# Routed experts on one core: where expert 0's ids are stored, where expert 1's rows are transposed, the order of the output rows, and how two items of the dense layer share TensorE

## The chip, the cores and the metric

The program runs on one core of a Trainium2 chip. The metric is the device time of one execution in microseconds; the kernel before was timed three times, and the median is used. One further execution was recorded by the hardware profiler, and everything read from a trace comes from that one.

## The reference

The reference has three stages, and only the last one is returned.

1. Attention over 4 batches, 8 heads, 576 positions and 64 values per head, with a causal window of 64 positions.
2. A mixture of 8 experts over the 2304 tokens of 512 values. Each token goes to exactly one expert and each expert takes exactly 288 tokens: the pairs of token and expert are walked in order of falling gate logit, and a pair is taken if the token is free and the expert is not full. Expert e computes `max(x @ w1[e], 0) @ w2[e]`, with 1024 hidden values.
3. A dense layer over all tokens: `h = x @ w_in` with 2048 hidden values, `g = max(0.01 * h, h)` (a leaky ReLU), and `g @ w_out`.

## The kernel before

**Stages.** Attention writes its rows to a scratch tensor in DRAM (`xd`). Then a router works in eight phases: phase ph finds the next expert to be filled and the ids of its 288 tokens (`r_ids`, three columns of 96). A phase is a long chain of small VectorE operations and small matmuls (tile `rp`): six rounds of a search for a threshold, and then the ids. "Expert 0" below is the one that phase 0 finds, and so on.

**Items.** Everything after the attention is one list of items, `seq`: expert 0 and expert 1 (8 items each, one per 128 hidden values), block m0 of the dense layer (16 items, one per 128 hidden values, over 512 slots), experts 2 and 3, m1, experts 4 and 5, m2, experts 6 and 7, m3, and m4 with the last 256 slots. A slot is a place in the order expert by expert: expert n fills slots 288n to 288n+287. So m2 (slots 1024 to 1535) needs only the first 96 slots of expert 5, and m3 (1536 to 2047) only the first 32 of expert 7. Expert outputs are kept transposed in `Y`, a ring of 1024 slots in two halves of 512, each with four tiles of 128 features. Where an expert's slots cross from one half into the other, `parts` (line 533) cuts them in two.

**Precision.** Each float is held as two parts, high and low, and a product is made of three matmuls: high by high, low by high, high by low. ScalarE writes the high part (a cast) and VectorE the low part (a subtraction). So for an item of the dense layer `hprod` issues 12 matmuls (4 feature tiles by 3), of which 4 read the low part of `Y`; `hstep` issues what is left of the 12 and then the activation; `ystep` issues the item's second product. Expert 0 alone works on whole floats, in 4 matmuls per step.

**Order.** The loop in `run` (line 877) writes every engine's instructions in program order: at item i the first product of item i+1 (`hstep(i + 1)`), then the second product of item i (`ystep(i)`). Weights come by `load_raw` (SyncE's queue; five buffers `raw`) and `split` (high and low part, two items ahead). A model of the engines' clocks (`Clocks`, line 973) decides, at each `tick` between matmuls, which pieces of the router's phase and of the conversion of the dense layer's weights (`Convert`, line 546) are written next. Engines run their own queues in order.

**From expert 0 to expert 1.** `gather_x(1)` issues three indirect loads of 96 rows each on GpSimd (tiles `xg`), and `xtrans(1, a)` transposes one of them on TensorE into `xtp`, from which ScalarE writes the high part and VectorE the low part of `xT`. The tile that `a = 0` and `a = 2` use is the same buffer. In this kernel all of that is written after expert 0's last second product (`ystep(7)`): in the branch `elif i + 1 == first[1]` of `run` come `R.finish(1)`, the gather, three loads on GpSimd's queue, three splits, the three transposes and `lows()` (the low parts of expert 0's output). The earlier branch, with the transposes two items ahead, is taken only if the ids are there by item 5.

**Ids for the output.** `put_ids(n)` (line 705) stores expert n's 288 ids, 4 bytes each, to the DRAM tensor `idl` by SyncE's queue, at item 4 of the expert (lines 910 and 911). Each block of the dense layer loads 512 of them at its ninth item, for the scatter of its output rows.

**End of an expert.** In `ystep`, `rows(0)` writes the high parts of the expert's output to `Y`, part by part and feature tile by feature tile, and `rows(1)` the low parts. The parts are sorted by falling length (line 828).

**Start of a block.** After an expert, `run` writes 8 products of the block's first item (none of them reads a low part of `Y`), then `PAIR` = 6 products of the second item, then the last 4 of the first item with its activation, then the other 6 of the second item, and then the first item's second product (`oa`), which reads the activation's result.

Of the kernel before, what the change touches and what calls it, by code (L numbers as in the profile page):

```python
# [623 lines left out]

FORCE, LEAD = 4, 10
XM = 4, 3, 2
PAIR = 6
ELOW, MLOW = 1, 1
WARM, CVG = 11, 2
XW = 5200  # L630
class Moe:
# [163 lines left out]
    def ystep(self, i):  # L795
        nc = self.nc
        kind, n, p, f = self.seq[i]
        self.route.flush(i)
        if kind == "m" and i == len(self.seq) - 2:
            return  # L800
        w, hh = self.w[i, 1], self.h[i]
        last = 7 if kind == "e" else 15
        st, sp = p == 0, p == last
        if kind == "e":
            if st:
                self.acc = [self.pp.tile([128, 288], F32, tag="acc", name=f"ya{n}_{d}", bufs=4) for d in range(4)]
            def prods(low):
                if n == 0:
                    for d in range(4):
                        nc.tensor.matmul(self.acc[d], w[:, 128 * d:128 * d + 128], hh[:, 0, :288].bitcast(F32), start=st, stop=sp)  # L810
                        self.route.tick()
                    return
                whi, wlo = w[:, 0], w[:, 1]
                for d in range(4):
                    a, b = whi[:, 128 * d:128 * d + 128], wlo[:, 128 * d:128 * d + 128]
                    for x, r in ((a, 0), (b, 0), (a, 1)):
                        if low is None or low == r:
                            nc.tensor.matmul(self.acc[d], x, hh[:, r, :288], start=st and x is a and r == 0, stop=sp and r == 1)
                    self.route.tick()
            if ELOW and not sp and n:  # L820
                prods(0)
                prods(1)
            else:
                prods(None)
            if sp:

                cut = [(s - 288 * n, pos, c) for s, pos, c in parts(288 * n, 288)]
                cut.sort(key=lambda x: -x[2])
                def rows(low, acc=self.acc):
                    for s, pos, c in cut:  # L830
                        for d in range(4):
                            hi, lo = (y[d][pos // 512][:, pos % 512:pos % 512 + c] for y in self.Y)
                            src = acc[d][:, s:s + c]
                            if low:
                                nc.vector.tensor_tensor(out=lo, in0=src, in1=hi.bitcast(F32), op=ALU.subtract)
                            else:
                                nc.scalar.copy(hi, src)
                rows(0)
                if n:
                    rows(1)  # L840
                else:

                    self.lows = lambda: rows(1)
        else:
            s0, N = self.mslots(n)
            nt = N // 128
            if st:
                self.acc = [self.pp.tile([128, 512], F32, tag="acc", name=f"oa{n}_{t}", bufs=4) for t in range(nt)]
            if p == 8:
                idx = self.wk.tile([128, 4], I32, tag="sidx", name=f"sidx{n}")  # L850
                nc.sync.dma_start(idx[:, :nt], self.idl[s0:s0 + N, :].rearrange("(t p) o -> p (t o)", p=128))
                self.sidx = idx
            if MLOW and not sp:
                for low in range(2):
                    for t in range(nt):
                        self.oprod(i, t, low)
                        if t % 2 or low == 0:
                            self.route.tick()
                return
            for t in range(nt):  # L860
                if i == len(self.seq) - 1:
                    self.oprod(i - 1, t)
                self.oprod(i, t)
                self.route.tick()
                if sp:
                    o = self.conv.pool.tile([128, 2, 512], F32, tag="cv_in", name=f"ot{n}_{t}", bufs=4)[:, 0, :]
                    if t % 2 == 0:
                        nc.vector.tensor_copy(o, self.acc[t])
                    else:
                        nc.scalar.copy(o, self.acc[t])  # L870
                    nc.gpsimd.memset(self.spacer, 0.0)
                    sc = nc.gpsimd.indirect_dma_start(out=self.out, out_offset=bass.IndirectOffsetOnAxis(ap=self.sidx[:, t:t + 1], axis=0), in_=o, in_offset=None)
                    for q in self.scats:
                        self.tc.declare_no_dep(sc.ins, q.ins, reason="rows of other tokens")
                    self.scats.append(sc)

    def run(self):
# [3 lines left out]
        def known():  # L881
            self.conv.hold = True
            for i in range(2):
                self.load_raw(i)
        R.finish(0, known)
        self.gather_x(0)
        for i in range(2, 5):
# [16 lines left out]
        for i in range(n):  # L904

            R.goal = 2 * (i - 16 + LEAD)
            nxt = seq[i + 1] if i + 1 < n else None
            yfirst = nxt is not None and nxt[2] == 0 and seq[i][0] == "e"
            R.goal = min(R.goal, 32)
            if seq[i][0] == "e" and seq[i][2] == 4:  # L910
                self.put_ids(seq[i][1])
            for m in range(1, 8):
                if m == 1 and not (self.ng == 2 and self.soon or 'ids' in R.out.get(1, ()) and i <= first[1] - 3):
                    continue
                self.soon |= m == 1
                if i == first[m] - FORCE and m > 1:
                    R.finish(m)
                if m == self.ng and 'ids' in R.out.get(m, ()) and i >= first[m - 1]:
                    self.gather_x(m)
                    self.ng += 1  # L920
                for a in range(3):
                    if i == first[m] - XM[a] and seq[i][0] == "m":
                        self.xtrans(m, a)
                if i == first[m] - 1 and seq[i][0] == "e":
                    self.xtrans(m, 2)
            if i == 2:

                self.conv.hold = False
                while len(self.conv.st) < 3:
                    self.conv.load()  # L930

            for j in range(i + 1, i + 6 if self.ng > 1 else min(i + 6, first[1] + 2)):
                self.load_raw(j)
            if yfirst:
                self.ystep(i)
                if i + 1 == first[1] and self.soon:
                    self.lows()
                elif i + 1 == first[1]:

                    R.finish(1, lambda: [self.load_raw(j) for j in range(i + 1, i + 3)])  # L940
                    self.gather_x(1)
                    self.ng = 2
                    for j in range(i + 3, i + 6):
                        self.load_raw(j, nc.gpsimd)
                    for j in range(i + 1, i + 3):
                        self.split(j, 0)
                    self.split(i + 1, 1)
                    for a in range(3):
                        self.xtrans(1, a)
                    self.lows()  # L950
                self.split(i + 3, 0)
                self.split(i + 2, 1)
                if PAIR and nxt[0] == "m":

                    self.hprod(i + 1, 8)
                    self.hprod(i + 2, PAIR)
                self.hstep(i + 1)
            else:
                self.split(i + 3, 0)
                self.split(i + 2, 1)  # L960
                if i + 1 not in self.h:
                    self.hstep(i + 1)
                if i == n - 3:
                    self.hstep(i + 2)
                x = [m for m in first if m > 1 - self.soon and first[m] == i + 2]
                if x and seq[i][0] == "e":
                    self.xtrans(x[0], 0)
                    self.xtrans(x[0], 1)
                self.ystep(i)
# [75 lines left out]
class RouteDriver:  # L1045
# [4 lines left out]
    EARLY, SPARE = 150, 700  # L1050
    def __init__(self, nc, router, conv):
        self.nc, self.r, self.conv, self.out, self.ph, self.g = nc, router, conv, {}, 0, None
        self.ready, self.mode, self.nfill, self.jobs, self.goal = 0, 'd', 0, [], 0
    def lighter(self):

        nc = self.nc
# [1 line left out]
    def piece(self):  # L1058
# [5 lines left out]
        try:  # L1064
            self.mode, self.nfill = next(self.g)
            self.ready = self.nc.last + self.FWD
        except StopIteration:
            self.g = None
            self.ph += 1
# [127 lines left out]
```

## Time and profile before

| what | value |
|---|---|
| times of three runs | 853.68, 855.95, 858.48 us; median 855.95 us |
| profiled execution | 850.8 us; its span from first to last instruction is 849.1 us |
| VectorE busy | 487.2 us (57%) |
| ScalarE busy | 316.2 us (37%) |
| GpSimd busy | 127.4 us (15%) |
| mean granted TensorE clock | 0.974 |

The span starts with the first instruction. The attention ends about 120 us into it, expert 0 runs from about 155 us, expert 1 from about 202 us, m0 from about 235 us, m1 from 397 us, m2 from 564 us, m3 from 708 us. Times of rows are us from the start of the span. A row of the timeline shows a run of like instructions: its start, how long it took, engine, operation, output and inputs, and in brackets the idle time before it and what ended that. Ends of matmuls are modelled, so that the next matmul may start before the end shown.

### The profile page before, as it was taken

The numbers are of one execution on the slowest core, as the hardware profiler recorded it, in microseconds if no ns is written. First come the engines' busy times: TensorE is split into PE (matmuls) and PEld (weight loads), VectorE is DVE, ScalarE is ACT, GpSimd is POOL, SyncE is SP. The second block draws the span as 40 slices with busy tenths as digits, with TensorE's granted clock in tenths as the row PEclk, the third lists the DMA queues.
The fourth block names the chain that finished last, engine by engine and source line by source line (L and its number), as shares of the span: only waits on it lengthen the run. The fifth ranks groups of instructions, "written<-read, shape, count | busy, mean of one in ns | idle before, by whom it ended". The sixth has DMA issues, their size and how long they took to land.

```text
span 849.1 us, 15411 instructions
## 1 busy us (share of the span) xinstructions
PE 795.3 (94%) x5877; PEld 654.7 (77%) x5877; DVE 487.2 (57%) x1381; ACT 316.2 (37%) x707; POOL 127.4 (15%) x147
## 2 busy tenths in 40 slices
PE   6998873998999999999999999999999999999996
PEld 4766652577977778888777778988888998888895
DVE  3799888577776877878665685322223322222332
ACT  3677742125225754342211134531124452212222
POOL 2111110210010001100000008620003770000100
PEclk9999985898999999999999999999999999999999
DMA  9999822478014985936314327581343935323662
GB/s 289 315 315 262 281 76 76 127 167 273 12 29 150 343 306 176 161 109 208 94 50 149 102 98 151 179 223 52 124 159 114 230 79 216 99 100 107 241 199 99
DMA packets 47417, 138.78 MB, mean 163 GB/s; under 512 B 10096, under 2 KB 10736, under 8 KB 47344
## 3 DMA queue, kind: packets, MB, share of 16 engines
q1 hardware_dynamic: 43072, 124.79, 47.9%
q0 software_dynamic: 3840, 12.59, 4.6%
q8 instruction: 46, 0.75, 0.5%
q10 hardware_dynamic: 432, 0.43, 0.1%
q14 instruction: 27, 0.22, 0.1%
HBM read 117.85 MB, written 19.93 MB: 162 GB/s over the span
## 4 chain that ended last, share of the span: by engine, by line
PE 51%; issue 5%; DMA 5%; DVE 5%; ACT 2%; POOL 0%; POOLq 0%; SPq 0%; DVEq 0%; ACTq 0%
PE h L1042 24%; PE oa L1042 17%; PE ya L1042 7%; PE rp L1042 2%; DMA xg<-xd,r_ids 1%; DMA idl<-r_ids 1%; DVE w L1042 1%; DMA out_dram<-ot,sidx 1%; PE xtp L1042 1%; DVE h L1042 1%; DVE hh L1042 1%; DMA sidx<-idl 1%; DMA w<-wsp 0%; DMA raw<-in_w_dram 0%; DVE r_ob L1042 0%
## 5 line engine op out<-in xcount | busy, mean ns | idle before, releaser
L1042 PE MATMUL h<-Y,w 128*128 128x512 f32 (+1 forms) x600 | 138.6, 376 | 0.0
L1042 PE MATMUL oa<-w,hh 128*128 128x512 f32 x540 | 135.0, 394 | 0.0
L1042 DVE SCALAR_TENSOR_TENSOR h<-h,tg 128x512 f32<-128x512 f32 (+1 forms) x80 | 51.5, 644 | 138.8 <-ACT tg L1042 138.4
L1042 ACT COPY tg<-h 128x512 f32<-128x512 f32 (+1 forms) x80 | 43.5, 544 | 218.0 <-PE h L1042 218.0
L1042 PEld LDWEIGHTS h<-Y,w 128*128 128x128 f32 x600 | 104.0, 188 | 20.6
L1042 PEld LDWEIGHTS oa<-w,hh 128*128 128x128 f32 x540 | 99.5, 188 | 20.8
L1042 PE MATMUL h<-xT,w 128*128 128x288 f32 x672 | 103.5, 302 | 0.6 <-ACT xT L1042 0.6
L1042 PE MATMUL ya<-hh,w 128*128 128x288 f32 x672 | 100.1, 297 | 0.5 <-DVE hh L1042 0.5
L1042 PEld LDWEIGHTS h<-xT,w 128*128 128x128 f32 x672 | 94.6, 192 | 2.7 <-issue 0.9
L1042 PEld LDWEIGHTS ya<-hh,w 128*128 128x128 f32 x672 | 91.7, 188 | 0.9 <-DVE hh L1042 0.7
L1042 PE MATMUL h<-Y,res 128*128 128x512 f32 (+1 forms) x360 | 83.6, 376 | 1.1 <-ACT Y L1042 1.1
L1042 PE MATMUL oa<-res,hh 128*128 128x512 f32 x324 | 82.1, 397 | 2.1 <-ACT hh L1042 2.1
L1042 ACT ACTIVATE hh<-h 128x288 fp32r<-128x288 f32 (+1 forms) x64 | 26.3, 411 | 132.9 <-PE h L1042 129.3
L1042 PEld LDWEIGHTS h<-Y,res 128*128 128x128 f32 x360 | 62.4, 188 | 14.0 <-ACT Y L1042 1.6
L1042 POOL TENSOR_TENSOR w<-raw,w 128x512 fp32r<-128x512 f32 x45 | 56.8, 1288 | 107.9 <-ACT w L1042 107.9
L1042 DVE TENSOR_TENSOR hh<-h,hh 128x512 fp32r<-128x512 f32 (+1 forms) x80 | 50.9, 637 | 37.6 <-ACT hh L1042 37.6
L1042 PEld LDWEIGHTS oa<-res,hh 128*128 128x128 f32 x324 | 59.3, 188 | 16.0 <-ACT hh L1042 3.8
L1042 POOL DMA_INDIRECT out_dram<-ot,sidx x18 | 18.4, 1022 | 333.1 <-DVE ot L1042 126.4
L1042 ACT CAST hh<-h 128x512 fp32r<-128x512 f32 (+1 forms) x80 | 43.5, 544 | 64.3 <-DVE h L1042 64.3
L1042 ACT CAST w<-raw 128x512 fp32r<-128x512 f32 x112 | 63.9, 619 | 2.0 <-DMA raw<-in_w_dram 2.0
L1042 DVE SCALAR_TENSOR_TENSOR hh<-h,hh 128x288 fp32r<-128x288 f32 x56 | 25.3, 454 | 53.4 <-ACT hh L1042 53.2
L1042 POOL DMA_INDIRECT xg<-xd,r_ids x24 | 26.7, 1113 | 146.5 <-DVE r_ac L1042 136.3
(150 smaller groups left out, 965.7 us busy)
## 6 DMA issues: line engine op xcount, KB each, us to landing
w<-wsp SPq DMA_DIRECT2D x80, 512.0 KB, 4.4
raw<-in_w_dram SPq DMA_DIRECT2D x58, 512.0 KB, 5.0
cv_in<-in_wio_dram SPq DMA_DIRECT2D x32, 512.0 KB, 6.3
wsp<-w SPq DMA_DIRECT2D x20, 512.0 KB, 3.8
aq<-in_q_dram SPq DMA_DIRECT2D x12, 384.0 KB, 6.2
avt<-in_vt_dram SPq DMA_DIRECT2D x12, 384.0 KB, 6.8
xd<-ax SPq DMA_DIRECT2D x18, 256.0 KB, 3.9
ak<-in_k_dram SPq DMA_DIRECT2D x8, 512.0 KB, 5.8
```

The lines of the kernel that those rows point to most:

```text
L1042: return f(*a, **kw)
```

## The change

- Expert 0's ids are stored at item 4 of expert 1, and expert 1's own at its item 6; the other experts' stay at their item 4.
- As soon as phase 1 has its ids, a hook in `RouteDriver.piece` writes the gather of expert 1's rows. If that has happened by item 6, three splits of expert 1's weights follow the first product of item 7, two transposes are written ahead of `ystep(6)`, the third ahead of `ystep(7)`, and `lows()` right after `ystep(7)`. Items 10 to 12 are then loaded by SyncE's queue and not by GpSimd's.
- The parts of an expert's output are written in the order of the slots and not by length.
- `PAIR` is 2 and not 6: 8 products of the first item, 2 of the second, 4 of the first, 10 of the second.

```diff
-PAIR = 6
+PAIR = 2
@@ in ystep
-                cut.sort(key=lambda x: -x[2])
+                cut.sort()
@@ in run
+        def rows():
+            self.gather_x(1)
+            self.ng = 2
+        R.hook = rows
         R.finish(0, known)
@@
-            if seq[i][0] == "e" and seq[i][2] == 4:
-                self.put_ids(seq[i][1])
+            if seq[i][0] == "e" and seq[i][1] and seq[i][2] in (4, 6):
+
+                if seq[i][2] == 4 or seq[i][1] == 1:
+                    self.put_ids(0 if seq[i][1] == 1 and seq[i][2] == 4 else seq[i][1])
             for m in range(1, 8):
-                if m == 1 and not (self.ng == 2 and self.soon or 'ids' in R.out.get(1, ()) and i <= first[1] - 3):
+                if m == 1 and not self.soon:
                     continue
-                self.soon |= m == 1
@@
+            if i == first[1] - 2:
+
+                self.hstep(i + 1)
+                self.soon = self.ng == 2
+                self.split(i + 2, 0)
+                self.split(i + 2, 1)
+                self.split(i + 3, 0)
             if yfirst:
@@ in the branch for ids that are not there
                     R.finish(1, lambda: [self.load_raw(j) for j in range(i + 1, i + 3)])
-                    self.gather_x(1)
-                    self.ng = 2
@@
-                if i + 1 not in self.h:
+                if i + 1 not in self.h and i != first[1] - 2:
                     self.hstep(i + 1)
@@ in RouteDriver.piece
             self.ready = self.nc.last + self.FWD
+            if self.hook and self.ph == 1 and 'ids' in self.out.get(1, ()):
+                self.hook()
+                self.hook = None
```

## Rows read from the trace of the kernel before

**Rows 1.** The profile's page, busy time of the engines (share of the span, instructions).
```profile
PE 795.3 (94%) x5877; PEld 654.7 (77%) x5877; DVE 487.2 (57%) x1381; ACT 316.2 (37%) x707; POOL 127.4 (15%) x147
```
**Rows 2.** Waits of TensorE, whole span: us in total, times, longest.
```profile
PE oa L1042 <- ACT hh L1042: 2.1, 4, 0.6
...
PE xtp L1042 <- DMA xg<-xd,r_ids: 1.6, 2, 1.0
...
PE h L1042 <- ACT Y L1042: 1.1, 2, 0.6
```
**Rows 3.** Timeline of TensorE from expert 0's last items to expert 1's first.
```profile
193.25 0.65 PE L1042 MATMUL ya<-hh,raw 128*128 128x288 f32 x2
...
193.94 3.66 PE L1042 MATMUL ya<-hh,raw 128*128 128x288 f32 x14
197.53 0.75 PE L1042 MATMUL rp<-r_oh,r_ge 128*63 128x8 bf16 x18
198.21 0.88 PE L1042 MATMUL xtp<-cft,xg 96*128 96x96 f32 x8
201.00 0.90 PE L1042 MATMUL xtp<-cft,xg 96*128 96x96 f32 x4 [1.91 <-DVE xT L1042]
202.47 5.57 PE L1042 MATMUL h<-xT,w 128*128 128x288 f32 x24 [0.57 <-ACT xT L1042]
207.88 1.35 PE L1042 MATMUL ya<-hh,w 128*128 128x288 f32 x9
```
**Rows 4.** Timeline of TensorE from expert 5's last item into m2.
```profile
560.51 3.32 PE L1042 MATMUL ya<-hh,w 128*128 128x288 f32 x24
564.38 2.13 PE L1042 MATMUL h<-Y,res 128*128 128x512 f32 x8 [0.55 <-ACT Y L1042]
...
568.68 1.56 PE L1042 MATMUL h<-Y,w 128*128 128x512 f32 x6
570.87 3.03 PE L1042 MATMUL oa<-res,hh 128*128 128x512 f32 x12 [0.63 <-ACT hh L1042]
```
**Rows 5.** Two stretches: busy time of each engine, then TensorE's granted clock (PEclk), DMA share, GB/s.
```profile
204.00:205.00 1.00, 1.00 (x6) 1.00 (x5) 1.00 (x4) 0.00 (x0) 0.00 (x0) 0.50 0.06 25
360.00:362.00 2.00, 0.98 (x7) 0.56 (x6) 1.83 (x7) 0.89 (x2) 0.00 (x0) 1.00 1.00 307
```
**Rows 6.** Timeline of ScalarE and of VectorE between the two experts.
```profile
197.93 1.66 ACT L1042 CAST w<-raw 128x512 fp32r<-128x512 f32 x3
199.50 0.86 ACT L1042 CAST xT<-xtp 128x384 fp32r<-128x384 f32 x2
...
198.59 1.89 DVE L1042 TENSOR_TENSOR w<-raw,w 128x512 fp32r<-128x512 f32 x3 [1.40 <-ACT w L1042]
200.40 1.01 DVE L1042 TENSOR_TENSOR xT<-xtp,xT 128x384 fp32r<-128x384 f32 x2
```
**Rows 7.** Timeline of GpSimd, the first gather of expert 1's rows.
```profile
186.99 0.98 POOL L1042 DMA_INDIRECT xg<-xd,r_ids  x1 [33.05 <-DVE r_ac L1042]
```
**Rows 8.** DMA issues in windows at 177, 182, 187 and 151 us: KB, us to landing.
```profile
idl<-r_ids SPq DMA_DIRECT2D x1, 1.1 KB, 10.5
...
raw<-in_w_dram SPq DMA_DIRECT2D x1, 512.0 KB, 9.3
...
xg<-xd,r_ids POOLq DMA_INDIRECT x1, 9.0
...
xg<-xd,r_ids POOLq DMA_INDIRECT x1, 3.2
```
**Rows 9.** Timeline of ScalarE and VectorE at the same crossing: the parts of expert 5's output.
```profile
562.68 2.07 ACT L1042 CAST Y<-ya 128x192 fp32r<-128x192 f32 x8 [1.57 <-PE ya L1042]
...
564.36 1.81 DVE L1042 TENSOR_TENSOR Y<-ya,Y 128x192 fp32r<-128x192 f32 x8 [2.75 <-ACT Y L1042]
```
**Rows 10.** Timeline of TensorE late in m0: two rounds of the router's phase 3.
```profile
316.91 0.61 PE L1042 MATMUL rp<-r_oh,r_ge 128*31 128x8 bf16 x18
...
322.96 0.61 PE L1042 MATMUL rp<-r_oh,r_ge 128*31 128x8 bf16 x18
```

More of the change, by code (lines that the diff above doesn't have):

```diff
@@ L1052, in __init__ @@
         self.nc, self.r, self.conv, self.out, self.ph, self.g = nc, router, conv, {}, 0, None
-        self.ready, self.mode, self.nfill, self.jobs, self.goal = 0, 'd', 0, [], 0
+        self.ready, self.mode, self.nfill, self.jobs, self.goal, self.hook = 0, 'd', 0, [], 0, None
     def lighter(self):
```

## The prediction

> **What bounds the kernel now.** I read the page first: TensorE is busy for 94% of the span, VectorE for 57% [rows 1]. So only what leaves TensorE idle, or slows it, can be won. Next the waits of TensorE: the blocks' second products wait four times for the activation, 2.1 us in all; the blocks' first products wait twice for rows of `Y`, 1.1 us; transposes wait for a gather, 1.6 us [rows 2]. Then its timeline where experts 0 and 1 meet [rows 3]: after expert 0's last product come eight transpose matmuls, 1.91 us of idling, four more, 0.57 us idle, and then the first products of expert 1, 24 matmuls from 202.47 to 207.88, 5.41 us. The same number of matmuls of 288 columns takes 3.32 us elsewhere [rows 4]. The granted clock explains that: 0.50 at 204 us [rows 5], the lower level of 1.2 GHz, after the idle stretch. So this one crossing costs its waits and about 2.1 us of half clock.
>
> **Expert 0 to expert 1, the sum.** From 193.25 (start of item 6's second product) to 207.88 (expert 1's first `ya`) are 14.63 us [rows 3]. The work in it at full clock: two second products 193.25 to 197.53, 4.28; router matmuls 197.53 to 198.21, 0.68; 12 transpose matmuls at 0.88 for eight, 1.3; 24 products, 3.3 by the row of block m2's crossing. Together 9.6, so at most 5.1 us can go.
>
> What is late next: the third transpose reuses the buffer of the first, so it waits until ScalarE and VectorE have read that. TensorE wants it at 193.25 + 0.9 + 2.1 = 196.3. ScalarE first has item 7's ReLU (about 0.4, from the page's table) to about 193.9, three weight casts (1.66), then the row casts (0.43 each): first rows cast at 196.0 [rows 6]. VectorE has three weight subtractions (0.63 each), the last after the last cast, to 196.2, then 0.5 for the rows: 196.7 [rows 6], and the release makes it near 197. I take a wait of 0.9. Bounds: 0 if VectorE is early; 3.3 if the three subtractions stay where the router's pieces leave VectorE free, at 197.2, and end at 199.1, the rows at 199.6. In the second case the clock falls as it does now and nothing is won. The value taken is nearest to the ScalarE rows, since that queue is nearly empty there. Gain: 5.1 - 0.9 = 4.2 us, between 0 and 5.1.
>
> **The gather itself** does not start earlier: GpSimd began it at 186.99 already [rows 7], right after the ids, since its queue was empty; the hook changes only where it is written. What changes is its landing. It took 9.0 us; expert 0's gather took 3.2; the weights issued at 182 took 9.3; and before them, at 177, SyncE issued the 288 ids, 10.5 us for 1.1 KB [rows 8]. I read the slow landings as the ids' store in front of them. Without it the first gather should land near 190.2 and the other two, issued 1.3 us apart, by 193, before the transposes at 193.3. If the store is not the cause, they land at 196 to 198 and hold TensorE for about 3 us.
>
> The two stores moved into expert 1 go out after its last weight load in SyncE's queue, so what lies behind them are loads for the conversion, wanted in m0. I cost them at nothing; if a weight load were behind them, it would be about 6 us late (9.3 against 3.2, the undisturbed gather, as the nearest row).
>
> **Loads of items 10 to 12** move from GpSimd's queue to SyncE's, where each waits for a buffer that expert 0's items 5 to 7 release, the last at about 199. Behind them wait the conversion's loads and items 13 to 15; item 10 is wanted near 204. Nothing, unless a landing takes over 9 us again; then up to 2 us. Splits and `lows()` are the same instructions in another order: nothing by themselves.
>
> **Order by slot.** It changes only experts 5 and 7 (96 slots then 192; 32 then 256); in experts 1 and 3 the needed part is the longer one and stands first already. At m2 the ScalarE casts run from 562.68, one per feature tile as TensorE finishes it; the four long ones go first and the fifth, which m2 needs, is done at about 564.3, so that TensorE idles 0.55 [rows 4, 9]. With the short ones first the needed four end with the last tile, and the wait goes. m3 repeats it. Gain: the 1.1 us of [rows 2].
>
> VectorE's first subtraction began at 564.36, 1.68 us after the first cast, though it needs only that one [rows 9]: it began when the fifth cast, the second on the same accumulator, was done. The Trainium skill, "PSUM — Partial Sum Buffer", section "PSUM bank collisions raise a hardware error", says that two engines must not read one bank at the same time, and that a dependency is put between them. By that rule, and the trace agrees, the low part for m2 cannot move forward with the order; by the order of the code alone it would start 1.3 us earlier. The sum is the same by both, since ten products cover it either way (next); by the rule the cover is thinner.
>
> **PAIR 2.** Before the first product that reads a low part stand 10 matmuls and not 14. At m2, from 563.8, at 2.13 us for eight, that is 2.6 us, to 566.4; the four short subtractions, 0.23 each from 564.36, and held by the eighth cast at 564.75, end near 565.3. So no wait, with 1 us to spare; at m3 the long casts are longer, some 0.5. Ten products (2.6 us at the six's 1.56) then stand between the first item's end and its second product instead of six, and the chain tg, leaky ReLU, high part takes 570.87 - 568.68 = 2.19 us [rows 4]. So the wait goes: 2.1 us over the four blocks [rows 2]. Bounds: if VectorE is behind at a block's start (m0 and m1 have the router beside it), the four products no longer in front cost up to 1 us a block, 4 in all, which is -1.9 net; nothing in the rows of m2 says so.
>
> Reported waits count from modelled ends, which overlap the next start by 0.07 in [rows 3]; six places, 0.4 us more. Blocks: 2.1 + 1.1 + 0.4 = 3.6 us.
>
> **Sum.** 4.2 + 3.6 = 7.8 us. The profiled execution took 850.8 us (span 849.1 and 1.7 around it), which gives 843.0; it lies 5.15 below the median 855.95, so for the median I take the difference: 848.
>
> **Rivals.**
> 1. *The clock stays low.* The tail of expert 0 is now cut by transposes and a wait of about 1 us. At 360 to 362 TensorE idled half of 2 us and the clock stayed at 1.00 [rows 5], against it; for it, the idle stretch at 199 to 202. Then 2.1 us stay: 850. The Trainium skill, "TensorE: Matmul & The Clock Gate", section "A second HAM failure mode: psum-queue depth-cycling", describes short idles between groups of matmuls that bring the clock down; by that rule it would be 850, and the row speaks for 848.
> 2. *A router round slips.* VectorE's pieces move, and phase 3 loses its place in m0, where rounds come 6.05 us apart late in the block [rows 10]. Its ids feed expert 3's gather, for which transposes wait already (longest 1.0 us, [rows 2]). One round late gives back up to 6: 854. Against it: everything behind expert 0 moves together.
> 3. *The crossing yields nothing:* the landings stay at 9 us, or the planner writes the ids after item 5 and takes the old branch. Then only the blocks gain: 852.
> 4. *The low parts come late* at the blocks, and their gain goes: 855.95 - 4.2, about 852.
> 5. *Slower.* Expert 0's outputs now stand behind transposes, and these behind gathers and behind weights that ScalarE casts first. If the last of these lands at L, expert 1's first `ya` starts at L + 0.9 + 4.3 + 0.4 + 0.7 + 5.4 (low clock) = L + 11.7. That equals today's 207.88 at L = 196.2, uses up the blocks' 3.6 at 199.8, and is slower by over 0.5% from 204.1. With two landings of 10.5 in a row, L = 208: 864. Against it: the 9.0 of [rows 8] gave 196.0.
>
> **How the numbers follow.** Chances: forecast 0.47 (845.5 to 850.5), rivals 1 to 5 in order 0.12, 0.15, 0.13, 0.07, 0.06. Three runs lie within 4.8 us, so that 0.5% (4.3 us) is about what can be told from no change. Faster by more than that, under 851.7: forecast and rival 1, 0.59, and 0.06 from the lower ends of 3 and 4: 0.65. Slower by more: rival 5 and a double slip in 2: 0.07. Within: 0.28. The range: below, all bounds at their best (5.1 + 4.3) and some of the spread of runs, 843.5; above, rivals 2 to 4 and little of 5, 857.
>
> **What would show it.** Crossing: transposes of expert 1 between expert 0's `h` and `ya`, under 1.5 us of idling, clock 1.00 at expert 1's first products and these in some 3.3 us; gathers landing in 3 to 4 us. Blocks: no wait of `oa` for `hh`; at m2 and m3 none of `h` for `Y`; a new one would be `h` for VectorE's `Y`. Wrong if the clock row still has 0.50, if the wait moves to `xtp` or to `ya`, or if expert 3's transposes wait longer than 1 us.

## The result, and the profile after

The changed kernel took 847.77 us (median of 19 runs, 841.43 to 852.67) beside 854.81 us for the kernel before (19 runs, 851.21 to 861.1): a ratio of 0.991 [0.9887, 0.9932], 7.0 us less where 7.8 were forecast. Run again on two other occasions it stood at a ratio of 0.9896 and 0.9885.

The profiled execution of the changed kernel is one of its longer ones (850.83 us, span 849.2), and that of the kernel before (850.8, span 849.1) one of its shorter ones. So the two pages show the same span, and busy shares say nothing here:

```profile
PE 797.7 (94%) x5876; PEld 657.9 (77%) x5877; DVE 488.3 (58%) x1381; ACT 316.8 (37%) x707; POOL 122.1 (14%) x144
```

What the change did is read stretch by stretch. In the rows, `h` is the output of a first product, `ya` of an expert's second product, `oa` of a block's second product, `xtp` of a transpose and `rp` of the router's matmuls; "half clock" means a granted clock of 0.50. TensorE's timeline where experts 0 and 1 meet (start, duration, count, idle time before), which answers to [rows 3]:

```profile
194.02 0.75 PE L1052 MATMUL h<-xT,raw 128*128 128x288 f32 x2
194.61 0.82 PE L1052 MATMUL xtp<-cft,xg 96*128 96x96 f32 x8
195.27 0.68 PE L1052 MATMUL ya<-hh,raw 128*128 128x288 f32 x2
195.88 0.18 PE L1052 MATMUL rp<-r_sat,pow 63*128 63x8 bf16 x1
195.99 1.72 PE L1052 MATMUL ya<-hh,raw 128*128 128x288 f32 x6
198.24 0.55 PE L1052 MATMUL xtp<-cft,xg 96*128 96x96 f32 x4 [0.53 <-DVE xT L1052]
198.62 2.13 PE L1052 MATMUL ya<-hh,raw 128*128 128x288 f32 x8
200.38 3.58 PE L1052 MATMUL h<-xT,w 128*128 128x288 f32 x24
203.80 1.75 PE L1052 MATMUL ya<-hh,w 128*128 128x288 f32 x12
```

The transposes stand between expert 0's last `h` and its last two `ya`; one wait of 0.53 is left of 1.91 and 0.57; the 24 first products of expert 1 take 3.42 us to the next start and not 5.41. From 194.61 to 203.80 are 9.19 us. A router round that stood in the 14.63 of before comes later now (0.68 us), so like stands against like at 9.87. The clock, in the columns of [rows 5]:

```profile
200.00:201.00 1.00, 1.00 (x8) 0.84 (x7) 0.86 (x5) 0.83 (x3) 0.00 (x0) 1.00 1.03 418
202.00:203.00 1.00, 1.00 (x9) 1.00 (x8) 1.00 (x4) 0.47 (x2) 0.00 (x0) 1.00 0.94 373
```

1.00 where it was 0.50. The engines that write the rows (ScalarE, then VectorE), against [rows 6]:

```profile
195.17 1.65 ACT L1052 CAST w<-raw 128x512 fp32r<-128x512 f32 x3
196.72 0.86 ACT L1052 CAST xT<-xtp 128x384 fp32r<-128x384 f32 x2
```
```profile
195.82 1.90 DVE L1052 TENSOR_TENSOR w<-raw,w 128x512 fp32r<-128x512 f32 x3 [0.93 <-ACT w L1052]
197.63 1.01 DVE L1052 TENSOR_TENSOR xT<-xtp,xT 128x384 fp32r<-128x384 f32 x2
```

The order is the one the working assumed: three weights, then the rows. Last, TensorE from expert 5 into m2, against [rows 4], with the casts and subtractions of [rows 9] behind it:

```profile
563.56 3.32 PE L1052 MATMUL ya<-hh,w 128*128 128x288 f32 x24
566.71 2.02 PE L1052 MATMUL h<-Y,res 128*128 128x512 f32 x8
568.57 0.63 PE L1052 MATMUL h<-Y,w 128*128 128x512 f32 x2
569.04 1.10 PE L1052 MATMUL h<-Y,res 128*128 128x512 f32 x4
569.97 2.50 PE L1052 MATMUL h<-Y,w 128*128 128x512 f32 x10
572.31 0.86 PE L1052 MATMUL oa<-res,hh 128*128 128x512 f32 x3
```
```profile
565.73 0.24 ACT L1052 CAST Y<-ya 128x96 fp32r<-128x96 f32 x1 [1.56 <-PE ya L1052]
...
566.91 1.13 ACT L1052 CAST Y<-ya 128x96 fp32r<-128x96 f32 x5 [0.16 <-PE ya L1052]
```
```profile
567.41 1.99 DVE L1052 TENSOR_TENSOR Y<-ya,Y 128x96 fp32r<-128x96 f32 x8 [2.75 <-ACT Y L1052]
```

No idle time is left. From the start of the expert's last products to the first `oa`, 10.36 us became 8.75. VectorE's first subtraction starts 1.68 us after the first cast, as before: the low part did not move forward with the new order.

### The profile page after: what moved, and what is told of

Its sections match the earlier page's. It is cut to its first block, busy times and chain, and to the rows that moved or that the text cites. A ratio compares the mean times of both kernels' runs of the same rounds, so it can differ in the third digit from the quotient of the medians.

```text
span 849.2 us, 15404 instructions
## 1 busy us (share of the span) xinstructions
PE 797.7 (94%) x5876; PEld 657.9 (77%) x5877; DVE 488.3 (58%) x1381; ACT 316.8 (37%) x707; POOL 122.1 (14%) x144
## 4 chain that ended last, share of the span: by engine, by line
PE 45%; issue 13%; DVE 4%; DMA 3%; ACT 1%; another core or an unknown queue 1%; POOL 0%; POOLq 0%; SPq 0%; DVEq 0%; ACTq 0%
PE h L1052 21%; PE oa L1052 13%; PE ya L1052 8%; PE rp L1052 2%; DMA xg<-xd,r_ids 1%; DMA sidx<-idl 1%; DMA out_dram<-ot,sidx 1%; PE xtp L1052 1%; DVE w L1052 1%; DVE r_ob L1052 1%; ACT w L1052 0%; DVE h L1052 0%; DVE hh L1052 0%; ACT cv_r L1052 0%
## 5 line engine op out<-in xcount | busy, mean ns | idle before, releaser
L1052 PE MATMUL ya<-hh,w 128*128 128x288 f32 x672 | 103.8, 302 | 0.4 <-issue 0.4
L1052 PEld LDWEIGHTS ya<-hh,w 128*128 128x128 f32 x672 | 94.4, 193 | 0.9 <-issue 0.6
L1052 DVE TENSOR_TENSOR w<-raw,w 128x512 fp32r<-128x512 f32 x67 | 44.1, 698 | 6.1 <-ACT w L1052 4.7
```

Of the source, the lines that this page charges most:

```text
L1052: return f(*a, **kw)
```

## The experiments

All times are medians beside the kernel before of the same occasion: 849.74 us for the first four rows, 853.8 for the next four, 853.25 for the last four. The ratios with their 95% intervals are not quotients of these medians, so that the two can differ by some 2 us.

| kernel | us (range, runs) | ratio to before | span of its profile |
|---|---|---|---|
| again | 841.54 (839.43 to 843.64, 6) | 0.9896 [0.9869, 0.9923] | 840.0 |
| crossing | 845.93 (844.56 to 850.36, 12) | 0.9967 [0.9947, 0.9986] | 843.3 |
| blocks | 847.92 (841.73 to 851.16, 12) | 0.9966 [0.9942, 0.999] | 849.5 |
| ids_late | 839.92 (839.15 to 841.02, 6) | 0.9875 [0.985, 0.99] | 838.9 |
| ids_back | 846.61 (844.29 to 852.09, 8) | 0.9931 [0.9902, 0.9959] | 850.4 |
| ids_only | 852.87 (850.64 to 857.16, 12) | 1.0 [0.9975, 1.0026] | 852.9 |
| length | 846.49 (843.5 to 851.17, 7) | 0.9917 [0.9889, 0.9945] | 849.5 |
| pair0 | 842.62 (839.94 to 844.78, 6) | 0.9886 [0.9856, 0.9916] | 838.3 |
| again2 | 842.63 (842.28 to 846.23, 6) | 0.9885 [0.9849, 0.9921] | 844.6 |
| ids_late2 | 842.48 (839.3 to 849.21, 10) | 0.9901 [0.9864, 0.9938] | 839.1 |
| ids_twice | 847.66 (845.19 to 854.13, 11) | 0.9945 [0.9917, 0.9973] | 849.1 |
| best | 840.39 (838.14 to 845.55, 6) | 0.9851 [0.9813, 0.9889] | 843.9 |

**The two halves.** `again` is the changed kernel; `crossing` is it without the edits at the blocks, `blocks` the kernel before with those alone.

```
crossing:  PAIR = 6;  cut.sort(key=lambda x: -x[2])
blocks:    PAIR = 2;  cut.sort()      (in the kernel before)
```

> The changed kernel once more, for a second trace. Theory (the prediction's sum): expert 0's tail to expert 1's first second product takes 9 to 10 us, 14.6 before; no wait for the activation or for rows of Y at the four blocks; the time is 7 to 8 us below that of before, and the 5 us that TensorE lost in expert 4 in the first trace (515 to 525 us) are chance and don't come again. Rival: expert 3 (2 us) and expert 4 (5 us) give back because of the change, by its other order of the router's pieces; then both losses stand in this trace too, and the time is about 1 us below that of before in a run without the other luck.

> The changed kernel with PAIR 6 and the parts in the order of their length, so that only the ids' stores and the transposes ahead are left of the change. Theory: crossing 9 to 10 us for 14.6, all four waits for the activation and both for rows of Y as before, 4 to 5.5 us less than before (ratio 0.994). Rival (a router round slips, what is won is given back at expert 3): ratio 0.999 and transposes of expert 3 that wait 3 us or more.

> The kernel before with the order by slot and PAIR 2 alone. Theory: the four waits for the activation and the two for rows of Y go, 3.6 us less (ratio 0.996), and the crossing from expert 0 to expert 1 is as before, 14.6 us with the clock at 0.50. Rival (low parts late): a new wait of the first products for VectorE's low part at m0 or m1, and a ratio of 1.000.

TensorE's timeline of `crossing`:

```profile
193.92 0.83 PE L1052 MATMUL xtp<-cft,xg 96*128 96x96 f32 x8
...
199.68 3.57 PE L1052 MATMUL h<-xT,w 128*128 128x288 f32 x24
203.09 1.75 PE L1052 MATMUL ya<-hh,w 128*128 128x288 f32 x12
```

and of `blocks`:

```profile
200.40 0.88 PE L1042 MATMUL xtp<-cft,xg 96*128 96x96 f32 x8
203.20 0.62 PE L1042 MATMUL xtp<-cft,xg 96*128 96x96 f32 x4 [1.92 <-DVE xT L1042]
204.39 5.89 PE L1042 MATMUL h<-xT,w 128*128 128x288 f32 x23 [0.57 <-ACT xT L1042]
```

The short crossing (9.17 us) is there with the one half, the long one (1.92 and 0.57, half clock) with the other. At the blocks it is the other way round. From the start of an expert's last second product to the first `oa`, read off the four timelines:

| | m0 | m1 | m2 | m3 |
|---|---|---|---|---|
| before | 9.53 | 10.10 | 8.78 | 8.78 |
| crossing | 8.89 | 10.11 | 8.79 | 8.79 |
| blocks | 8.74 | 9.31 | 7.18 | 7.18 |
| again | 8.88 | 9.33 | 7.18 | 7.17 |

At m1 to m3 the edits give 0.8, 1.6 and 1.6 us. At m0 router pieces stand in between and shift: 8.89 there without the edits, so that theirs is between nothing and 0.8. By the times, the halves give 3.8 and 1.8 us (2.8 and 2.9 by the ratios), together less than the 8.2 of `again` (8.8 by the ratio), but the intervals are too wide to say that the halves fail to add up; the profile of `blocks` has waits of 1.71 and 0.95 us at expert 3's transposes, and half clock behind them, which belongs to none of its edits (below).

**The store and the transposes, apart.** `ids_back` keeps the transposes forward but stores the ids as before; `ids_only` is the kernel before with the store moved.

```diff
 ids_back
-            if seq[i][0] == "e" and seq[i][1] and seq[i][2] in (4, 6):
-                if seq[i][2] == 4 or seq[i][1] == 1:
-                    self.put_ids(0 if seq[i][1] == 1 and seq[i][2] == 4 else seq[i][1])
+            if seq[i][0] == "e" and seq[i][2] == 4:
+                self.put_ids(seq[i][1])
 ids_only: the same lines the other way round, in the kernel before
```

> The changed kernel with every expert's ids stored at its own item 4 again, expert 0's too; the rest of the change stays. Theory (the store holds back what is issued behind it): the weights of items 8 and 9 and the gathers of expert 1's rows land some 9 us after their issue, at 196 to 198, so that the transposes ahead of expert 0's outputs wait about 3 us for them, the clock falls to 0.50 again at expert 1's first products, and 4 to 5 us of the crossing's gain are lost: about 846 where the changed kernel has 841.5. Rival (the gather was slow for other loads beside it): landings as in the changed kernel, and the same time within 1 us.

> The kernel before with the ids of experts 0 and 1 alone stored later (items 4 and 6 of expert 1). Theory: the gathers land within 5 us, but nothing in the old order waits for them (the crossing waits for ScalarE's and VectorE's work on the transposes), so the crossing stays at 14 to 14.6 us with the clock at 0.50, and the time is that of before (ratio 1.000, within 0.002). Rival (moving the store is itself what pays): ratio 0.995 or less.

DMA issues from 176 to 206 us (count, KB each, median us to landing) of `ids_back`, `ids_only` and `again`:

```profile
xg<-xd,r_ids POOLq DMA_INDIRECT x3, 7.7
idl<-r_ids SPq DMA_DIRECT2D x1, 1.1 KB, 10.9
```
```profile
xg<-xd,r_ids POOLq DMA_INDIRECT x3, 5.6
```
```profile
xg<-xd,r_ids POOLq DMA_INDIRECT x3, 3.3
```

With the store in front the gather takes 7.7 (8.7 in the kernel before and 9.5 in `blocks`, same window), without it 5.6 and 3.3. TensorE's timeline of `ids_back`:

```profile
194.22 0.75 PE L1050 MATMUL h<-xT,raw 128*128 128x288 f32 x2
197.13 0.55 PE L1050 MATMUL xtp<-cft,xg 96*128 96x96 f32 x4 [2.17 <-DMA xg<-xd,r_ids]
198.20 0.52 PE L1050 MATMUL xtp<-cft,xg 96*128 96x96 f32 x4 [0.51 <-ACT xT L1050]
...
199.28 3.25 PE L1050 MATMUL ya<-hh,raw 128*128 128x288 f32 x6
...
204.58 3.58 PE L1050 MATMUL h<-xT,w 128*128 128x288 f32 x24
208.00 1.22 PE L1050 MATMUL ya<-hh,w 128*128 128x288 f32 x8
```

The transposes wait 2.17 us for the gather, and the clock falls, but earlier: six `ya` take 3.25 us where the changed kernel has 1.72, and the 24 products are at full speed again. The windows of `ids_back` say the same:

```profile
201.00:202.00 1.00, 1.00 (x4) 0.70 (x3) 0.00 (x0) 0.00 (x0) 0.00 (x0) 0.50 0.99 365
204.00:205.00 1.00, 1.00 (x6) 0.79 (x6) 0.86 (x6) 0.80 (x3) 0.00 (x0) 1.00 0.74 262
```

The crossing is 13.2 us (from where the transposes were wanted, near 194.8, to 208.00), 4.0 longer than in the changed kernel, and the time of 846.61 is the one expected. In `ids_only` all transposes still come last, the third waits 1.92 us for VectorE, and the time is the kernel before's:

```profile
201.49 0.80 PE L1044 MATMUL xtp<-cft,xg 96*128 96x96 f32 x4 [1.92 <-DVE xT L1044]
```

So the store's move alone is worth nothing here, and the transposes' move without it some 0.8 us at this place (13.2 and the router's 0.68, against 14.63); they pay together. Both figures for the place come from one execution each; the time of `ids_back`, 5.9 us under the kernel before by its ratio, fits them (0.8 here and the 4.0 to 4.8 of the blocks).

**Inside the blocks.** `length` keeps PAIR 2 and takes the order by slot back; `pair0` puts no product of the second item in front.

```
length:  cut.sort(key=lambda x: -x[2])
pair0:   PAIR = 0;  if nxt[0] == "m":      (instead of: if PAIR and nxt[0] == "m":)
```

> The changed kernel with the parts in the order of their length. Theory: TensorE waits 0.55 us for rows of Y at m2 and at m3 again, 1.4 to 1.6 us more than the changed kernel by the timeline, nothing else; about 843. Rival (with two products in front only, the low parts of the short piece, now last, come late too): a wait of the first products for VectorE's Y at m2 as well, and 3 us more or over.

> The changed kernel with no product of a block's second item ahead of the first item's last four (8, 4, 12 and not 8, 2, 4, 10). Theory: the low parts are there just in time (at m3 VectorE's last one ends about 1.8 us after TensorE's first product, which is what eight products take), so waits of 0 to 0.3 us a block and the same time as the changed kernel within 1 us. Rival (the cover of two products is needed): first products wait for VectorE's Y at all four blocks, 1 to 3 us more in all.

Waits of TensorE in `length`:

```profile
PE h L1052 <- ACT Y L1052: 1.1, 2, 0.6
```

The old wait is back twice, and m2 and m3 take 8.00 each. So of the 1.60 per block 0.78 are PAIR's (8.78 to 8.00) and 0.82 the order's (8.00 to 7.18). `pair0` has 7.17 and 7.18 at m2 and m3, no wait for a low part, and a time that can't be told from the changed kernel's: the two products in front are not needed as cover. `length` took 3.9 us more than `pair0`, over the 1.6 of the blocks and in the range that its rival named, though the intervals overlap; the rival's sign, a wait for VectorE's `Y`, is not there, but 3.95 us of idling at expert 3 are (next).

**What varies from run to run.** The profile of the changed kernel spent its gain at three places. Expert 0's first `ya` was 1.4 us later than in the kernel before, at half clock for longer. Around expert 3's transposes, ahead of expert 2's last second products, TensorE waited and then had half clock:

```profile
356.58 0.16 PE L1052 MATMUL rp<-r_sat,pow 63*128 63x8 bf16 x1 [1.29 <-DVE r_sat L1052]
...
359.05 0.52 PE L1052 MATMUL xtp<-cft,xg 96*128 96x96 f32 x4 [1.05 <-DMA xg<-xd,r_ids]
359.35 3.03 PE L1052 MATMUL ya<-hh,w 128*128 128x288 f32 x12
```

In the kernel before, waits of 0.86 and 0.98 at the same place, the second of them ending at 362.04, left the clock at 1.00, from 360 to 362 [rows 5] and behind them:

```profile
362.00:364.00 2.00, 1.96 (x16) 1.99 (x17) 1.06 (x3) 0.48 (x1) 0.00 (x0) 1.00 0.96 356
```

And in expert 4 TensorE waited 1.5 us for nothing that the profile shows, then 1.9 for the router's VectorE piece, and had half clock after it:

```profile
PE rp L1052 <- DVE r_ob L1052: 2.3, 2, 1.9
PE h L1052 <- issue: 1.5, 2, 1.0
```

`again` lost 2.5 us at the first place and nothing at the others, and its span is 840.0. For expert 3 I suspected the store of expert 2's ids, issued at 338.97 just ahead of weights and gather. `ids_late` moves the stores of experts 2, 4 and 6 as the change moved expert 0's:

```diff
-            if seq[i][0] == "e" and seq[i][1] and seq[i][2] in (4, 6):
-                if seq[i][2] == 4 or seq[i][1] == 1:
-                    self.put_ids(0 if seq[i][1] == 1 and seq[i][2] == 4 else seq[i][1])
+            if seq[i][0] == "e" and seq[i][1] % 2 and seq[i][2] in (4, 6):
+                self.put_ids(seq[i][1] - (seq[i][2] == 4))
 (and eight buffers for the ids instead of three)
```

> The changed kernel with the ids of experts 2, 4 and 6 stored in the time of experts 3, 5 and 7 as well (and eight buffers for ids, so that the stores may be that late). Theory (a store of ids holds back what is issued behind it for some 10 us): the gather for expert 3 lands in 3 to 5 us and not 11 to 12, the wait of expert 3's transposes (1.0 us) goes and with it a chance of half clock there; 1 to 3 us less than the changed kernel. Rival (the gathers are slow for the weights beside them): the gather for expert 3 lands as late as now and nothing is won.

Three more runs beside a control followed: `ids_late` again, the three stores doubled, and the late stores together with PAIR 0 (`best`).

```
ids_twice:  for s0 in (288 * n, NTOK + 288 * n) if n in (2, 4, 6) else (288 * n,):
                self.nc.sync.dma_start(self.idl[s0:s0 + 288, :]...)
```

> The changed kernel once more, as the control of the three beside it. Both theories: some 7 us under the kernel before (its medians so far stand at ratios 0.991 and 0.990 to the kernel before). Theory S (what is left in front of expert 3 is the store of expert 2's ids): after that store, for about 10 us, the transfers move 20 to 50 GB/s, ScalarE waits 1 to 5 us for a weight, and TensorE idles 1 to 4 us ahead of expert 3's transposes. Theory R (a round of the router came late): expert 3's gather is issued later than in the kernel before.

> The kernel that also stores the ids of experts 2, 4 and 6 in the time of experts 3, 5 and 7, a second time. Theory S: no wait of TensorE ahead of expert 3's and expert 7's transposes but a release, no wait of ScalarE for a weight there, and 1.5 to 5 us under the changed kernel of this call, with a smaller spread of the runs (839.2 to 841.0 was the first time). Theory R: the same time as the changed kernel, since the router is untouched.

> The changed kernel with the ids of experts 2, 4 and 6 stored twice, the second time to unused rows; everything else is the same. Theory S: the 9 to 11 us in which little is moved behind each of these three stores become 18 to 22 us; two weights and the gather of expert 3 land 9 us later, and of that what is not covered shows: 4 to 8 us more idle ahead of expert 3's transposes, 2 to 6 us ahead of expert 5's and of expert 7's, together 8 to 18 us over the changed kernel, which makes it slower than the kernel before. Theory R: 1.1 KB more in a queue costs under 1 us each, and the time is the changed kernel's.

> The late stores and no product of the second item in front at a block (PAIR 0) together. Both theories: the second part alone was worth nothing that could be told (842.6 beside 841.5 to 847.8), so the time is that of the late stores alone, within 1.5 us; no wait of the second product for the activation at a block, and none of the first products for rows of Y.

The ten microseconds behind that store, in the changed kernel, then in `ids_late` (columns of [rows 5]):

```profile
340.00:350.00 10.00, 9.78 (x83) 9.23 (x82) 9.20 (x28) 4.16 (x9) 3.13 (x3) 1.00 1.14 84
```
```profile
340.00:350.00 10.00, 9.83 (x84) 9.27 (x83) 9.20 (x28) 4.06 (x9) 3.13 (x3) 1.00 0.69 202
```

84 GB/s against 202 (94 in `again`; 190 and 205 in the two other executions with the store moved), while the DMA engines show as more busy (1.14 against 0.69). The gathers of expert 3, in `again` and in `ids_late` (count, median us to landing):

```profile
xg<-xd,r_ids POOLq DMA_INDIRECT x3, 10.7
```
```profile
xg<-xd,r_ids POOLq DMA_INDIRECT x3, 4.0
```

In the changed kernel ScalarE then waits 2.4 us for a weight, in `length`, where TensorE idled 3.95 us at this place, 5.1; in `ids_late` and its repetition it does not wait, and TensorE has no wait there. Row of ScalarE's waits, 340 to 366 us, in `length`:

```profile
ACT w L1052 <- DMA raw<-in_w_dram: 5.1, 1, 5.1
```

The gather of expert 3 is issued at 345.16 in the changed kernel and at 348.68 before, so it moved forward with everything: no router round slipped. That the store slows what is issued behind it is shown, and TensorE waited for none of it in the three executions with the store moved. With the store in place the wait is anything from 0.2 (`ids_twice`) to 4.1 us (`ids_back`: 3.52 and 0.53), so a single one proves little. That the move shortens the kernel is not shown: 839.92 beside 841.54 on the first occasion, with intervals that overlap, and 842.48 beside 842.63 on the last. Doubling the store gave 5.0 us over the control (the intervals just overlap), less than the 8 to 18 expected, and only in part where expected: at expert 3 nothing was lost (78 GB/s in the ten microseconds from 342, 89 in the control), as if two stores in a row overlapped rather than added up. In the profile of `ids_twice` it was lost in expert 4, where VectorE's next write of ids waited for a store (6.2 us in `again`, with TensorE waiting for nothing behind it), and TensorE for what VectorE had behind it (waits from 505 to 532 us):

```profile
DVE r_ids L1053 <- DMA idl<-r_ids: 10.1, 1, 10.1
...
PE ya L1053 <- DVE hh L1053: 3.8, 1, 3.8
```

and ahead of expert 7, where the third transpose waited 1.54 us for VectorE and the clock fell to 0.50. `best` has the lowest median of all, 840.39, but its interval overlaps its neighbours'; its profile again has the loss in expert 4 (VectorE 1.0 us and TensorE 1.79 us for nothing shown, then half clock), with no store there:

```profile
513.67 0.54 PE L1050 MATMUL rp<-r_ob,r_rhs 128*6 128x96 bf16 x9 [1.79 <-issue]
```

So expert 4's loss does not need the store, and its cause stays open.

## Why the prediction was right

- *Crossing, 4.2 forecast.* 14.63 to 9.87 is 4.8 by the timeline of the changed kernel; from expert 0's first `ya` (162.57, and 163.93 in the changed kernel) to the end of the second product of expert 1's second item (the next start, 212.94 and 209.77), where both have done the same work, 50.37 us became 45.84, 4.5 less. The wait for the third transpose was 0.53 and not 0.9, within its bounds: ScalarE had the rows cast at 197.15 against 196.0 worked out, VectorE at 198.14 against 196.7, but TensorE had come 1.4 later as well.
- *The gather.* Forecast 3.2 us to landing without the store in front; 3.3 measured. `ids_back` is the alternative that the working gave, transposes held "for about 3 us": 2.17 and 0.51 and a fall of the clock.
- *Blocks, 3.6 forecast; mis-sized.* Measured 4.0 at m1 to m3, and up to 0.8 at m0. The order gave 1.6 instead of 1.1, PAIR 2 at m2 and m3 0.78 each instead of 0.63 and 0.62. The term that was too small is the 0.4 us for modelled ends. I took 0.07 of overlap per place; in the timeline of m2 above, a modelled end lies 0.16 or 0.17 past the next start (566.71 + 2.02 against 568.57). A reported wait of 0.55 hides that much, and the eight matmuls behind a wait took 2.13 instead of 2.02. Together 0.55 + 0.17 + 0.11 = 0.83, the 0.82 measured.
- *Low parts.* At m2 VectorE's first subtraction started at 567.41, with the end of ScalarE's fifth cast (567.05, 0.33 long), the second on the same accumulator, and 1.68 us after the first cast. The Trainium skill, "PSUM — Partial Sum Buffer", section "PSUM bank collisions raise a hardware error", says that two engines must not read one bank at the same time; the trace agrees. The cover was enough: no wait of `h` for VectorE's `Y` in the changed kernel, nor in `pair0`.
- *Rivals.* 1: no, the clock was 1.00 at expert 1. The fall it speaks of did come elsewhere, after expert 3's two short waits. 2: its sign was there, and it stood among the signs of being wrong (expert 3's transposes waited 1.05, over the 1.0 named; 0.98 in the kernel before), but not its mechanism: late weights and a slow gather behind a store, not a slipped round. 3: refuted by `crossing`. 4: refuted. 5: did not come about; `ids_back` is its mechanism at L = 197.13, and its first `ya` of expert 1 came at L + 10.9 where L + 11.7 was worked out.
- *The sum.* 4.5 and 4.0 to 4.8 make 8.5 to 9.3 by the traces. The medians gave 7.0, 8.2 and 10.6 on three occasions (7.7, 8.8 and 9.8 by the ratios), in which the places that vary from run to run come and go on either side. The forecast of 7.8 lies among them; that the first comparison came so near is no finer confirmation, since I had no term for those places and took 0.4 to 1.2 us too little for the blocks.

## What to carry to other kernels

The store of 288 ids of 4 bytes took SyncE 0.43 us to issue, and the gathers issued just behind it took 7.7 to 9.5 us to land where they took 3.3 to 5.6 without it. Whether the small elements or something else about the store does this was not tried. Put such a store where no load is soon wanted, and move it together with the work that wants the load, since at this crossing either move alone gave under 1 us and both 4.5. Size a wait by start-to-start distances with and without it, not by the reported idle time, which was short by a fifth to a third here. When a change is worth less than 1% and one profile disagrees with the times, compare starts of the same work down both traces: gains stay at their place, and what comes and goes elsewhere is not the change.

## What was not expected of the hardware

- Two idle stretches of about a microsecond near each other lowered the clock in one execution (1.29 and 1.05, then 0.50 at 360 us) and not in another (0.86 and 0.98, then 1.00 at 362 to 364).
- With the store of 288 elements of 4 bytes transfers went at 84 GB/s for ten microseconds, and at 202 with the store moved away; two such stores in a row cost little more of it than one (78 and 89 GB/s).
- Ahead of the fall in expert 4, engines waited for nothing that the profile shows: TensorE 1.5 us in the changed kernel, TensorE 1.8 and VectorE 1.0 in `best`. In `again` TensorE had none and no fall came; in `ids_twice` it had 1.15 at that place and the clock stayed at 1.00 to 525.
